# Loading q and k in 1 KB runs and putting the global keys inside the key chunks, in a banded attention followed by a hard-swish MLP

## The chip, the cores and the metric

The kernel runs on one core of a Trainium2 chip. The metric is device time in microseconds (us), the median of the executions of one kernel. An execution is also profiled; its span is about 1.7 us shorter than the device time of that same execution. The names of the engines are PE (TensorE, matmul), PEld (its weight loads), ACT (ScalarE), DVE (VectorE), POOL (GpSimd) and SP (SyncE, which here only issues DMA).

## The reference, cut to what matters

Eight batches, eight heads, 512 local positions and 32 global positions per head, head size 64. A local query sees all 32 global keys and the local keys within 32 positions of it. A global query sees all 544 keys. The attention's output (4352 rows of 512) goes through a two-layer MLP with 2048 hidden units, called MoE in the code and "expert" in some of the texts.

```python
s_g  = scale * q_g @ k_all.T                       # global queries: all keys
s_ll = where(|i - j| <= 32, scale * q_l @ k_l.T, -1e9)
s_lg = scale * q_l @ k_g.T
a_l  = softmax(concat(s_lg, s_ll));  out_l = a_l @ concat(v_g, v_l)
x    = concat(out_g, out_l)          # per batch: 544 rows of 512
h    = x @ w_in                      # 512 -> 2048
y    = (h * clip(h + 3, 0, 6) / 6) @ w_out
```

Inputs of the attention are drawn at 0.1 times a unit normal, so the scores are tiny and the softmax is nearly uniform. Some experiments below put rows in a wrong order on purpose; the comparison with the reference can't see that ("correct" there says nothing about order), and they serve for timing alone.

## The kernel before

One batch is four pairs of heads. For each pair the kernel transposes k and q on PE, copies them out of PSUM (k by DVE, q by ACT), computes band scores of four key blocks with query windows of 160, 192, 192 and 160 columns, and applies exp (ACT) and the band mask (DVE). A separate stage, once for two pairs, scores the global keys. Then V is applied, with the softmax's denominator in the upper 64 rows.

```python
def emit_T(p):
    ...                                            # 8 transposes by PE into psT (fp16 PSUM)
    nc.vector.tensor_copy(out=kT, in_=psT[:, 0:Sl])
    nc.scalar.copy(out=qT, in_=psT[:, Sl:2 * Sl])

def emit_G(Q):                                     # the global keys' score stage, two pairs at once
    for pp in range(2):
        nc.tensor.matmul(out=psA[:, 0:Sl], lhsT=kgz[:, b, m], rhs=st[p]["qT"], ...)
        nc.tensor.matmul(out=psB[:, 0:Sg], lhsT=kgz[:, b, m], rhs=qgT[:, m, b], ...)
    nc.scalar.activation(out=EG[:, 0:Sl], in_=psA[:, 0:Sl], func=EXP, scale=qk_scale)
    nc.scalar.activation(out=EG[:, Sl:S], in_=psB[:, 0:Sg], func=EXP, scale=qk_scale)
```

The MLP of one batch is cut into 32 units of work: 16 of the hidden layer (`u1`, tile `psH`, four matmuls of 512 columns each) and 16 of the output layer (`u2`, tile `po`). They fill PE while the next batch's attention waits for ACT and DVE. `M(n)` emits n of them.

```python
for p in range(NPAIR):
    ...
    emit_T(p + 2)
    M(1); emit_QK(p + 1); M(2); emit_G(...)        # G in every second pair
    M(2); emit_AV(p, lambda: M(1))
    if m == NM - 1:
        M(len(units))                              # finish this batch's units
        units += moe_units(...)                    # the next batch's 32
    else:
        M(2)
```

All PSUM tiles but one come from one pool of seven buffers. All loads of the local q, k and V are issued by POOL, and the DMA casts them from fp32 to fp16 on the way.

The softmax here doesn't subtract the row's maximum and nothing guards it: scores larger than these inputs give would overflow.

## Time and profile before

| | before |
|---|---|
| device time, median | 375.73 us (375.42 to 375.76) |
| span of the profiled execution, mean granted clock | 375.0 us, 0.986 |
| first matmul | 20.07 us |
| first hidden-layer matmul (psH); psH without gaps from | 44.7 us; 49.8 us |
| first output-layer matmul (po) | 70.4 us |
| one batch, psH to psH | 40.2 us: 20.9 hidden half + 19.3 output half |
| DMA packets | 114,272 |

I call "hidden half" the time from a batch's first psH matmul to its first po matmul, and "output half" the rest; both come from the timeline of PE.

The chain of waits, from the page of the kernel before (shares of the span, by engine and then by line; a q after an engine's name is its queue, "issue" is time in which it waited for nothing that the profile shows):

```profile
PE 62%; DVE 12%; POOL 9%; ACT 9%; issue 3%; DMA 3%; POOLq 0%
PE po L338 27%; PE psH L324 23%; PE pav L292 4%; ACT Rc L301 3%; DMA win_86<-in_moe_w_in_dram 3%; ACT Ln L298 3%; PE pav L284 2%; POOL kn L103 2%; POOL qn L103 2%; PE psGA L256 2%; POOL vn_81 L107 1%; POOL vgz L161 1%; PE pg L295 1%; POOL kn L96 1%; POOL qn L96 1%
```

PE's own MLP matmuls (po, psH) are half of it; POOL's issues (kn, qn, vn, vgz) are the start. The timeline of PE where the MLP begins (start, duration, engine, line, operation; in brackets the idle time before it and what ended it):

```profile
44.68 0.38 PE L324 MATMUL psH<-xt_324,win_84 128*128 128x512 f16 x1
45.93 0.39 PE L324 MATMUL psH<-xt_325,win_85 128*128 128x512 f16 x1 [0.87 <-DMA win_85<-in_moe_w_in_dram]
48.43 0.61 PE L324 MATMUL psH<-xt_326,win_86 128*128 128x512 f16 x1 [2.11 <-DMA win_86<-in_moe_w_in_dram]
```

The MLP is ready at 44.68 us and waits for the input weights. One batch of the steady part, by the windows view (window; its length; busy us and number of instructions of PE, PEld, DVE, ACT, POOL; granted clock; DMA share; GB/s):

```profile
130.00:170.20 40.20, 38.69 (x316) 20.57 (x313) 26.12 (x57) 28.46 (x56) 10.49 (x13) 1.00 0.69 66
```

PE is busy 38.69 of 40.20 us. It is the bound, with 1.5 us of idle time, and DVE and ACT have 14 and 12 us to spare over a whole batch. The groups that the change touches, with every shape apart (out<-in, shape, count; busy us, mean ns of one). A second group of 64 mask products (mask_79, 337 ns) is left out:

```profile
L244 DVE TENSOR_TENSOR E<-E,mask_80 128x352 f16<-128x352 f16 x64 | 20.9, 340 | 5.4 <-ACT E L242 3.4
L219 ACT COPY qT<-psT 128x512 f16<-128x512 f16 x32 | 18.8, 586 | 22.9 <-DVE kT L218 22.7
L218 DVE COPY kT<-psT 128x512 f16<-128x512 f16 x32 | 13.4, 418 | 2.9 <-PE psT L213 2.9
```

### The profile page before, as it was taken

Reading aid. Unit: us, or ns where it says so; the run is one execution under the profiler, and the core shown is the slowest. Engines: PE = TensorE matmul, PEld = TensorE weight load, DVE = VectorE, ACT = ScalarE, POOL = GpSimd, SP = SyncE. Lnnn points to the kernel's source line nnn. Section 1 sums busy time; section 2 is a strip of 40 time slices with the busy share of each in tenths; the row PEclk is TensorE's granted clock in tenths of the full one; section 3 lists DMA queues with packets and bytes.
Section 4 is the critical chain, followed back from the end, with each engine's and each line's share of the span. In section 5 each row is a group of like instructions: output and inputs, shape, how many; then the busy total and the mean of one; then the engine's idle time right before and its main releaser. Section 6 shows DMA issues by size and latency. Waiting matters only on the chain.

```text
span 375.0 us, 6707 instructions
## 1 busy us (share of the span) xinstructions
PE 332.3 (89%) x2608; PEld 178.9 (48%) x2608; DVE 235.6 (63%) x489; ACT 239.5 (64%) x473; POOL 102.6 (27%) x132
## 2 busy tenths in 40 slices
PE   0078589999999999999999999999999999999995
PEld 0046335555455554554555445545555445544472
DVE  7855667645875487548764587448754885296171
ACT  1059969745984599547965698458945895375070
POOL 8999436923240307003700343000000000000000
PEclk9998969999999999999999999999999999999999
DMA  9999999999390469119961949100001000100202
GB/s 131 120 77 141 199 204 169 152 131 84 44 101 29 75 67 110 32 58 86 68 47 56 114 27 86 50 36 30 2 30 56 30 2 28 58 28 0 87 29 56
DMA packets 114272, 27.44 MB, mean 73 GB/s; under 512 B 107328, under 2 KB 109376, under 8 KB 114240
## 3 DMA queue, kind: packets, MB, share of 16 engines
q0 software_dynamic: 104896, 17.05, 60.7%
q1 hardware_dynamic: 9344, 9.97, 7.9%
q8 instruction: 20, 0.33, 0.4%
q14 instruction: 12, 0.10, 0.1%
HBM read 35.13 MB, written 8.91 MB: 117 GB/s over the span
## 4 chain that ended last, share of the span: by engine, by line
PE 62%; DVE 12%; POOL 9%; ACT 9%; issue 3%; DMA 3%; POOLq 0%
PE po L338 27%; PE psH L324 23%; PE pav L292 4%; ACT Rc L301 3%; DMA win_86<-in_moe_w_in_dram 3%; ACT Ln L298 3%; PE pav L284 2%; POOL kn L103 2%; POOL qn L103 2%; PE psGA L256 2%; POOL vn_81 L107 1%; POOL vgz L161 1%; PE pg L295 1%; POOL kn L96 1%; POOL qn L96 1%
## 5 line engine op out<-in xcount | busy, mean ns | idle before, releaser
L298 ACT ACTIVATE Ln<-pav 64x512 f32<-64x512 f32 x64 | 37.9, 593 | 45.4 <-PE pav L292 38.1
L342 DVE COPY ot<-po 128x512 f32<-128x512 f32 x34 | 23.5, 692 | 25.6 <-PE po L338 25.2
L96 POOL DMA_DIRECT2D kn<-in_k_l_dram x28 | 24.7, 898 | 44.3 <-PE psT L213 36.5
L219 ACT COPY qT<-psT 128x512 f16<-128x512 f16 x32 | 18.8, 586 | 22.9 <-DVE kT L218 22.7
L96 POOL DMA_DIRECT2D qn<-in_q_l_dram x28 | 24.8, 926 | 6.7 <-PE psH L324 1.9
L284 PE MATMUL pav<-EG,vgz 128*128 128x512 f16 x64 | 24.7, 386 | 1.4 <-ACT qT L219 1.1
L244 DVE TENSOR_TENSOR E<-E,mask_79 128x352 f16<-128x352 f16 x64 | 19.8, 337 | 8.4 <-ACT E L242 8.2
L244 DVE TENSOR_TENSOR E<-E,mask_80 128x352 f16<-128x352 f16 x64 | 20.9, 340 | 5.4 <-ACT E L242 3.4
L324 PEld LDWEIGHTS <-win_86 128*128 128x128 f16 x144 | 14.2, 98 | 18.4 <-DMA win_86<-in_moe_w_in_dram 2.4
L324 PEld LDWEIGHTS <-win_87 128*128 128x128 f16 x144 | 14.1, 98 | 15.9 <-DMA win_87<-in_moe_w_in_dram 0.5
L301 ACT ACTIVATE Rc<-Ln 128x512 f32<-128x512 f32 x32 | 20.0, 626 | 0.7
L233 PEld LDWEIGHTS <-kT 64*128 64x128 f16 x256 | 13.6, 95 | 13.6 <-issue 13.1
L324 PEld LDWEIGHTS <-win_85 128*128 128x128 f16 x144 | 14.1, 98 | 11.0 <-issue 2.1
L112 POOL DMA_DIRECT2D vn_82<-in_v_l_dram x12 | 10.6, 918 | 31.4 <-PE pg L295 31.4
L190 PE MATMUL psGT<-ident,kgn_192 128*128 128x128 f16 x8 | 1.2, 304 | 20.1 <-DVE kgn_192 L183 20.1
L324 PEld LDWEIGHTS <-win_84 128*128 128x128 f16 x144 | 14.1, 98 | 9.8 <-issue 0.6
L238 PEld LDWEIGHTS <-kT 64*128 64x128 f16 x256 | 12.8, 94 | 6.7 <-issue 6.6
L218 DVE COPY kT<-psT 128x512 f16<-128x512 f16 x32 | 13.4, 418 | 2.9 <-PE psT L213 2.9
L286 PE MATMUL pg<-EG,vgz 128*128 128x32 f16 x64 | 10.8, 180 | 4.7 <-DVE xg_199 L314 4.7
L213 PE MATMUL psT<-ident,qn 128*128 128x128 f16 x128 | 12.9, 225 | 0.0
L112 POOL DMA_DIRECT2D vn_81<-in_v_l_dram x8 | 7.1, 909 | 21.1 <-PE pg L295 20.6
L213 PE MATMUL psT<-ident,kn 128*128 128x128 f16 x128 | 12.8, 225 | 0.0
(1097 smaller groups left out, 1112.3 us busy)
## 6 DMA issues: line engine op xcount, KB each, us to landing
out_dram<-ot SPq DMA_DIRECT2D x32, 256.0 KB, 2.0
kn<-in_k_l_dram POOLq DMA_DIRECT2D x28, 128.0 KB, 4.1
qn<-in_q_l_dram POOLq DMA_DIRECT2D x28, 128.0 KB, 5.3
vn_82<-in_v_l_dram POOLq DMA_DIRECT2D x12, 128.0 KB, 3.9
vn_83<-in_v_l_dram POOLq DMA_DIRECT2D x8, 128.0 KB, 5.1
vn_81<-in_v_l_dram POOLq DMA_DIRECT2D x8, 128.0 KB, 4.8
kgn<-in_k_g_dram SPq DMA_DIRECT2D x8, 64.0 KB, 2.7
kn<-in_k_l_dram POOLq DMA_DIRECT2D x8, 64.0 KB, 3.5
```

What stands on the lines that cost most here:

```text
L96: nc.gpsimd.dma_start(out=t[:, kb], in_=src[b, :, kb * P:(kb + 1) * P, :].rearrange("h s d -> s h d"))
L103: nc.gpsimd.dma_start(out=t[:, :, h], in_=src[b, h].rearrange("(kb p) d -> p kb d", p=P))
L112: nc.gpsimd.dma_start(out=vn[b % NV][:, kb, :, 0:D], in_=v_l[b, :, kb * P:(kb + 1) * P, :].rearrange("h s d -> s h d"))
L213: nc.tensor.matmul(out=psT[:, w * Sl + j * P:w * Sl + (j + 1) * P], lhsT=t[:, j, 2 * m:2 * m + 2].rearrange("p h d -> p (h d)"), rhs=ident ...
L219: nc.scalar.copy(out=qT, in_=psT[:, Sl:2 * Sl])
L244: nc.vector.tensor_tensor(out=E[:, e, half, 0:HALF], in0=E[:, e, half, 0:HALF], in1=mask[half], op=mult)
L284: nc.tensor.matmul(out=pav[:, 0:Sl], lhsT=vgz[:, b, h], rhs=EG[:, 0:Sl], start=True, stop=False, skip_group_check=True)
L298: nc.scalar.activation(out=Ln[e * D:(e + 1) * D], in_=pav[D:P, 0:Sl], func=LN)
L301: nc.scalar.activation(out=Rc, in_=Ln, func=EXP, scale=-1.0)
L324: nc.tensor.matmul(out=ps[:, 0:n], lhsT=w_in_t[m][:, c * P:(c + 1) * P], rhs=rhs(m), start=(m == 0), stop=(m == NM - 1))
L338: nc.tensor.matmul(out=po[t][:, 0:dm], lhsT=gts[c][:, t * P:(t + 1) * P], rhs=w_out_t[c // 4][:, c % 4], start=(c == 0), stop=(c == NC - 1))
L342: nc.vector.tensor_copy(out=ot, in_=po[t][:, 0:dm])
```

## The change

The intent is threefold. First, q and k are loaded as fp32 so that one partition reads four neighbouring rows, 1 KB in one run, in few DMA issues by SP, and are cast on chip; this is to bring the start forward. Row `4p + j` then lies in partition `p`, so the transposed copies out of PSUM have to put the rows back in order. Second, the keys are cut into five chunks of 128 with overlaps; chunk 1 holds the 32 global keys and serves queries 0 to 191, chunk 3 holds them again and serves queries 192 to 511, which ends the global score stage. Third, the global queries get one small 64-column matmul per chunk.

```diff
-        nc.vector.tensor_copy(out=kT, in_=psT[:, 0:Sl])
-        nc.scalar.copy(out=qT, in_=psT[:, Sl:2 * Sl])
+        nc.vector.tensor_copy(                      # the global keys, into two places of kT
+            out=kT[:, GC[0]:GC[0] + 2 * (GC[1] - GC[0])].rearrange(...)[:, :, 0:Sg],
+            in_=kgT[b % 2][:, m:m + 1].to_broadcast([P, 2, Sg]))
+        kv = psT[:, 0:Sl].rearrange("d (j p) -> d j p", j=J)            # J = 4
+        for k0, k1, c0 in SEG:                      # three pieces: 128, 160, 224 keys
+            nc.vector.tensor_copy(
+                out=kT[:, c0:c0 + k1 - k0].rearrange("d (p j) -> d j p", j=J),
+                in_=kv[:, :, k0 // J:k1 // J])
+        nc.scalar.copy(
+            out=qT.rearrange("d (p j) -> d j p", j=J),
+            in_=psT[:, Sl:2 * Sl].rearrange("d (j p) -> d j p", j=J))
 ... (scores)
+    CH = [(0, 0, 0, 160), (Sg, 128, 0, 192), (0, 160, 192, 128), (Sg, 288, 192, 320),
+          (0, 384, 352, 160)]            # globals in the chunk, first key, first query, queries
+        for c in range(NCH):
+            nc.tensor.matmul(out=psG[:, c * 2 * Sg:(c + 1) * 2 * Sg],
+                             lhsT=kT[:, KC[c]:KC[c] + P], rhs=qgz[b % 2][:, m])
 ... (emit_G is gone; the E masks have 480 columns instead of 352; Eg gets a mask of 128)
 ... (start)
+    for m in range(2):
+        for i, src in enumerate((k_l, q_l)):
+            load_rows(nc.sync, nat[0][0][i], src[0], 2 * m, 2)          # fp32, by SP
+        if m == 0:
+            load_g(0, gf0)
+    load_v0(0)                                                          # V as fp32, by SP
+    ...
+    for i in range(4):
+        load_w_in(i)                                                    # by POOL, at once
 ... (loop)
+        if b + 1 < B:                                # casts of the next batch: POOL, after the start
+            cast_rows(b + 1, m, first if b == 0 and m < 2 else pool)
```

## The prediction

> **What bounds the kernel now.** Granted clock 0.986, span 375.0 us, split by the first MoE matmuls of each batch (timeline of PE).
> - Start, 0 to about 50 us. PE does nothing until 20.07 us. The chain of waits runs there through POOL's DMA issues (kn, qn, vn: 0.69 to 0.74 us each, one after another); then batch 0's attention keeps ACT busy without a gap from 22.0 to 47.8 us, and the first MoE matmuls wait for win (11.94 us). The dense stream begins at 49.8 us.
> - Middle: one batch takes 40.2 us (psH of consecutive batches at 129.99 and 170.2). 512-column matmuls start every 0.216 us. By start times PE needs 128 x 0.216 = 27.65 for the MoE and, per pair, 0.45 (transposes) + 0.43 (scores; the two heads run side by side) + 0.24 (global scores) + 1.30 (AV) = 2.42: 37.3 in all. The other 2.9 us are stalls, mostly in the hidden half (20.9 us against 19.35 for the output half), where PE waits for DVE (gt, xg).
> - Tail: 45 us of pure MoE from 329.7 us, unchanged.
>
> **What the change does, costed.**
> 1. Start: q and k of two heads come in a few issues not made by POOL, V as fp32 likewise; win is queued at once. First exp near 9 us instead of 25. ACT then still needs, with start-to-start times from the trace (E 0.40 for 416 columns, so 0.45 for 480; qT 0.47; Ln 0.6; Rc 0.52) plus query casts, 23 to 25 us (kgz's 3.3 us are gone). DVE needs about as much. Dense MoE from 36 us (32 to 41): 14 us earlier, all on the critical path. Some 2 us more may come back in batch 0's hidden half, which runs now among win waits and a reduced clock (PEclk 0.83 at 40 to 60 us).
> 2. PE per pair: global scores 0.24 become five 64-column matmuls (0.14) and 0.05 of transposes; scores 0.43 to 0.41; AV 1.30 to 1.08 (960 columns against 1216). 2.42 becomes 2.13: 1.15 us a batch.
> 3. Added to DVE: the kT copy (418 ns) becomes three copies with an 8-byte step plus one of the global keys. The Trainium skill ("VectorE: DVE Perf Modes", "Mode 2×_1P") asks for 16-bit data at step 1; the trace agrees for the dense copy (418 ns against 692 for fp32). So 1x: an estimate of 1.0 + 0.2 us. Masks 352 to 480 columns: 0.34 to 0.40 each, plus one Eg mask of 0.2. DVE rises from 26 to 31 us a batch; in the hidden half it is nearly full, so it returns part of step 2.
> 4. POOL gets eight casts a batch, which share SBUF ports with DVE (the skill, "SBUF — State Buffer", "Who interferes with whom"). POOL has 28 us free a batch, so no wait for casts.
> 5. ACT: EG (0.62 + 0.24 per two pairs) out, Eg and wider E in: even.
>
> Net period 39.3 us (38.4 to 40.5): 6 us saved. DMA packets fall to about half.
>
> **Predicted**: 36 + 40.8 + 6 x 39.2 + 45.3 = 357 us, range 347 to 368. Faster by over 2%: 0.88; within 2%: 0.09; slower: 0.03.
>
> **What would show it.** First PE matmul near 7 us; dense psH from about 36 us, then batches 39.3 us apart; kT pieces 0.3 to 0.4 us each; E masks 0.40 us; DVE near 31 us per batch; POOL never on the chain after 40 us.
>
> **What would make it wrong.** Win loads starving the first k, q or V loads; POOL casts taking several us or blocking DVE's masks; DVE becoming the bound so the period stays at 40; or a start quicker than ACT's sum.

## The result, and the profile after

The changed kernel took 392.25 us (median, 391.86 to 392.92, 4 executions) against 375.75 us of the kernel before in the same rounds. The ratio is 1.0437, 95% interval 1.0413 to 1.046: slower. Ratios in this document are the mean time of one kernel's runs over that of the kernel before's of the same rounds, so they are not quite the ratios of the medians quoted.

| us | before | predicted | after |
|---|---|---|---|
| first matmul | 20.07 | 7 | 11.73 |
| first exp | 25.31 | 9 | 18.72 |
| first psH | 44.7 | 36 | 51.2 |
| from there to the next batch's psH | 45.1 | 40.8 | 45.8 |
| then six batches | 238.6 | 235.2 | 246.6 |
| rest | 46.6 | 45.3 | 46.9 |
| one steady batch | 40.2 | 39.3 | 41.5 |

The columns of measured pieces add up to the spans, 375.0 and 390.5. The prediction's pieces add up to 357.3, so it missed by 33 us: 15 until the first psH, 5 until the next batch's, 11 in the six batches and 2 in the rest. Against the kernel before, 7.2 us are lost until the second psH and 8.0 us in the six batches after it. The second loss is the plainer one. One batch of the steady part, windows view of the changed kernel:

```profile
138.50:180.00 41.50, 39.20 (x312) 21.31 (x310) 30.98 (x74) 32.34 (x58) 11.12 (x18) 1.00 0.51 95
```

DVE is 4.9 us busier in a batch, as predicted (31), but ACT is 3.9 us busier too, where "even" was predicted. The groups, with every shape apart:

```profile
L245 DVE TENSOR_TENSOR E<-E,mask 128x480 f16<-128x480 f16 x128 | 53.6, 439 | 17.9 <-ACT E L244 16.8
L215 ACT COPY qT<-psT 128x512 f16<-128x512 f16 x32 | 41.8, 1305 | 13.2 <-DVE kT L212 12.5 <-DVE mask L176 0.7
L212 DVE COPY kT<-psT 128x224 f16<-128x224 f16 x32 | 22.3, 697 | 0.0
L212 DVE COPY kT<-psT 128x160 f16<-128x160 f16 x32 | 17.6, 551 | 0.0
L212 DVE COPY kT<-psT 128x128 f16<-128x128 f16 x32 | 14.0, 439 | 5.2 <-PE psT L202 5.2
```

The same 512 elements of qT take 1305 ns instead of 586, four times a batch: 2.9 us of ACT's 3.9. The three kT pieces take 1.69 us together instead of 0.42.

The chain of waits of the changed kernel:

```profile
PE 41%; ACT 20%; DVE 17%; DMA 11%; issue 5%; SPq 5%; POOL 0%; ACTq 0%
PE po L317 28%; DMA gz_79<-in_k_g_dram 6%; PE psH L302 6%; DVE kT L212 4%; ACT qT L215 4%; ACT Ln L276 4%; SPq L137 4%; PE pav L272 3%; DVE gt L308 3%; DMA qf<-in_q_l_dram 3%; ACT Rc L279 2%; DMA vf<-in_v_l_dram 2%; ACT E L244 1%; SPq L94 1%; PE psT L202 1%
```

POOL has left the chain, as intended, but PE fell from 62% to 41%, with kT and qT copies and several loads in its place (gz are the global keys and queries, qf and vf are q and V as fp32). Three moments of the start show the loads (timelines of ACT, of POOL, and of PE):

```profile
4.34 0.62 ACT L125 CAST qr_142<-qf 128x512 f16<-128x512 f32 x1 [2.25 <-DMA qf<-in_q_l_dram]
15.26 0.62 ACT L125 CAST qr_147<-qf 128x512 f16<-128x512 f32 x1 [10.30 <-DMA qf<-in_q_l_dram]
...
18.72 0.52 ACT L242 ACTIVATE Eg<-psG 128x320 f16<-128x320 f32 x1
```

```profile
23.68 0.99 POOL L140 CAST vn_84<-vf 128x640 f16<-128x640 f32 x1 [17.96 <-DMA vf<-in_v_l_dram]
```

```profile
65.75 0.45 PE L187 MATMUL psGT<-ident,gz_79 128*128 128x32 f16 x8 [2.88 <-DMA gz_79<-in_k_g_dram]
```

The first q cast ran at 4.34 us, but the second, issued by SP at 3.30, waited until 15.26, and V until 23.68. Meanwhile the four win loads, queued by POOL from 1.35 us on, took their share. At 62.9 us PE, in the middle of a hidden half, stopped for the global keys of batch 2, which had been issued at 41.48 us behind the output weights and landed 24.2 us later.

### The profile page after: what moved, and what is told of

It is laid out like the page before. It is cut to its first block, busy times and chain, and to the rows that moved or that the text cites. A ratio compares the mean times of both kernels' runs of the same rounds, so it can differ in the third digit from the quotient of the medians.

```text
span 390.5 us, 6834 instructions
## 1 busy us (share of the span) xinstructions
PE 337.8 (87%) x2560; PEld 186.0 (48%) x2560; DVE 273.8 (70%) x628; ACT 270.4 (69%) x479; POOL 86.4 (22%) x134
## 2 busy tenths in 40 slices
DMA packets 72274, 36.82 MB, mean 94 GB/s; under 512 B 47408, under 2 KB 67888, under 8 KB 72240
## 4 chain that ended last, share of the span: by engine, by line
PE 41%; ACT 20%; DVE 17%; DMA 11%; issue 5%; SPq 5%; POOL 0%; ACTq 0%
PE po L317 28%; DMA gz_79<-in_k_g_dram 6%; PE psH L302 6%; DVE kT L212 4%; ACT qT L215 4%; ACT Ln L276 4%; SPq L137 4%; PE pav L272 3%; DVE gt L308 3%; DMA qf<-in_q_l_dram 3%; ACT Rc L279 2%; DMA vf<-in_v_l_dram 2%; ACT E L244 1%; SPq L94 1%; PE psT L202 1%
## 5 line engine op out<-in xcount | busy, mean ns | idle before, releaser
L317 PEld LDWEIGHTS <-gt 128*128 128x128 f16 x544 | 49.4, 97 | 54.1 <-issue 2.5
L245 DVE TENSOR_TENSOR E<-E,mask 128x480 f16<-128x480 f16 x128 | 53.6, 439 | 17.9 <-ACT E L244 16.8
L215 ACT COPY qT<-psT 128x512 f16<-128x512 f16 x32 | 41.8, 1305 | 13.2 <-DVE kT L212 12.5
L212 DVE COPY kT<-psT 128x128 f16<-128x128 f16 (+2 forms) x96 | 41.4, 562 | 5.2 <-PE psT L202 5.2
L317 PE MATMUL po<-wout_91,gt 128*128 128x512 f16 x136 | 35.0, 379 | 0.0
L317 PE MATMUL po<-wout_90,gt 128*128 128x512 f16 x136 | 34.9, 379 | 0.0
L317 PE MATMUL po<-wout_93,gt 128*128 128x512 f16 x136 | 34.9, 379 | 0.0
L317 PE MATMUL po<-wout_92,gt 128*128 128x512 f16 x136 | 34.9, 378 | 0.0
L239 PEld LDWEIGHTS <-kT 64*128 64x128 f16 x320 | 14.7, 98 | 24.8 <-issue 15.8
L242 ACT ACTIVATE Eg<-psG 128x320 f16<-128x320 f32 x32 | 14.1, 439 | 12.5 <-PE psG L229 12.4
L272 PE MATMUL pav<-E,vn_84 128*128 128x160 f16 (+3 forms) x160 | 22.1, 274 | 0.0
L272 PE MATMUL pav<-E,vn_85 128*128 128x160 f16 (+3 forms) x160 | 20.3, 244 | 0.0
L302 PEld LDWEIGHTS <-win_89 128*128 128x128 f16 x144 | 13.6, 98 | 13.6 <-issue 1.6
L272 PEld LDWEIGHTS <-vn_84 128*128 128x128 f16 x160 | 15.9, 108 | 7.9 <-issue 1.1
L302 PEld LDWEIGHTS <-win_86 128*128 128x128 f16 x144 | 13.5, 98 | 12.9 <-issue 0.9
L302 PEld LDWEIGHTS <-win_87 128*128 128x128 f16 x144 | 13.6, 98 | 12.0
L302 PEld LDWEIGHTS <-win_88 128*128 128x128 f16 x144 | 13.1, 97 | 12.2 <-issue 0.2
L274 PE MATMUL pg<-Eg,vn_84 128*128 128x32 f16 x160 | 13.3, 181 | 6.3 <-DVE vn_84 L140 4.3
L272 PEld LDWEIGHTS <-vn_85 128*128 128x128 f16 x160 | 14.7, 97 | 6.9
```

The source lines that it names most:

```text
L212: nc.vector.tensor_copy(out=kT[:, c0:c0 + k1 - k0].rearrange("d (p j) -> d j p", j=J), in_=kv[:, :, k0 // J:k1 // J])
L215: nc.scalar.copy(out=qT.rearrange("d (p j) -> d j p", j=J), in_=psT[:, Sl:2 * Sl].rearrange("d (j p) -> d j p", j=J))
L239: nc.tensor.matmul(out=pss[e][:, c0:c0 + nq], lhsT=kT[r, KC[c]:KC[c] + P], rhs=qT[r, q0:q0 + nq])
L242: nc.scalar.activation(out=Eg, in_=psG[:, 0:NCH * 2 * Sg], func=EXP, scale=qk_scale)
L245: nc.vector.tensor_tensor(out=E[:, e, t], in0=E[:, e, t], in1=mask[:, t], op=mult)
L272: nc.tensor.matmul(out=pav[:, q0:q0 + nq], lhsT=lhs, rhs=E[:, e, t, c0:c0 + nq], start=(i == 0), stop=(i == NCH - 1), skip_group_check=True)
```

## The experiments

Theory 1 (steady part): the loss of 1.3 us a batch comes from the copies that *write* SBUF with an 8-byte step. Its rivals are the wider masks, the casts on POOL, and the new matmul order. Theory 2 (start): the loads are bound by the DMA engines and in the wrong order. Its rivals are the clock, the dearer copies, and POOL's casts.

All results in one table (four executions each; "O" is the first po matmul, "batch" one steady batch; both from the profiled execution, which need not be the median one):

| run | median us | ratio to before, 95% | first psH | O | batch |
|---|---|---|---|---|---|
| after | 392.25 | 1.0437 (1.0413 to 1.046) | 51.2 | 77.5 | 41.5 |
| x_dense | 387.33 | 1.0315 (1.027 to 1.0359) | 45.9 | 78.5 | 40.4 |
| x_kdense | 389.57 | 1.0358 (1.0317 to 1.0399) | 50.0 | 78.2 | 41.0 |
| x_qdense | 387.56 | 1.0303 (1.0268 to 1.0338) | 48.8 | 77.5 | 40.7 |
| x_readstride | 386.16 | 1.0261 (1.0206 to 1.0317) | 48.0 | 79.3 | 40.3 |
| y_before_scatter | 393.22 | 1.0475 (1.0441 to 1.0509) | 51.9 | 74.1 | 42.1 |
| x_gz3 | 395.47 | 1.0506 (1.0448 to 1.0564) | 52.4 | 81.3 | 41.5 |
| x_read_gz3 | 377.87 | 1.0061 (1.0016 to 1.0105) | 46.8 | 70.6 | 40.3 |
| x_hold | 385.11 | 1.0272 (1.0208 to 1.0335) | 44.3 | 74.8 | 41.5 |
| x_hold_nopool | 385.48 | 1.0269 (1.0206 to 1.0333) | 45.6 | 69.8 | 41.5 |
| x_read_hold | 375.39 | 0.9985 (0.9942 to 1.0027) | 47.0 | 68.6 | 40.3 |
| x_read_hold_c1 | 376.09 | 1.001 (0.9961 to 1.006) | 48.2 | 70.5 | 40.3 |
| x_read_hold_c1_carry | 371.52 | 0.9892 (0.9867 to 0.9916) | 45.5 | 67.8 | 39.7 |
| x_first | 376.08 | 1.0025 (0.9977 to 1.0073) | 39.0 | 69.1 | 40.3 |
| x_first_split | 371.1 | 0.9885 (0.9853 to 0.9917) | 44.0 | 70.3 | 39.4 |
| x_first_split_carry | 368.19 | 0.9802 (0.9774 to 0.9831) | 44.2 | 69.8 | 39.1 |
| y_before_split | 368.11 | 0.9784 (0.9746 to 0.9822) | 45.0 | 67.3 | 39.0 |
| y_before_split_carry | 366.07 | 0.9749 (0.9722 to 0.9776) | 44.9 | 68.7 | 38.8 |

### Which side of the copy carries the step

x_dense writes and reads both copies densely. The rows then stand in the wrong order.

```diff
-                out=kT[:, c0:c0 + k1 - k0].rearrange("d (p j) -> d j p", j=J),
-                in_=kv[:, :, k0 // J:k1 // J])
+                out=kT[:, c0:c0 + k1 - k0], in_=psT[:, k0:k1])
-            out=qT.rearrange("d (p j) -> d j p", j=J), in_=psT[...].rearrange("d (j p) -> d j p", j=J))
+            out=qT, in_=psT[:, Sl:2 * Sl])
```

> The kernel after, with the kT and qT copies written densely, so the rows come out in the wrong order: the result is wrong on purpose. Nothing else changes. Theory S (the scattered 2-byte writes at an 8-byte step are what lengthened the period from 40.2 to 41.5 us): qT falls from 1.305 to 0.59 us, the three kT pieces from 1.69 us in all to about 0.8 us, the batch period to 39.3 to 39.7 us, the time from 392 to about 375 us (about 14 us in the middle, 2 to 3 us in the start). Rival W (the wider masks, POOL's casts on the shared port, or the smaller PSUM slack are the cause): the copies get shorter but the period stays above 41 us and the time above 387 us.

x_kdense and x_qdense do so for one copy alone.

> The changed kernel with the three kT pieces of VectorE written densely and ScalarE's qT copy still scattered (row order wrong on purpose). Theory V (VectorE's scattered pieces, about 1.2 us a pair dearer, lengthen the batch): period 41.5 to 40.4 to 40.7, as with both dense, time 386 to 389. Theory A (ScalarE's qT, 0.7 us a pair dearer, which the scores wait for): period stays 41.2 to 41.5, time 390 to 392.

> The changed kernel with ScalarE's qT copy written densely and VectorE's kT pieces still scattered (row order wrong on purpose). Theory V: period stays 41.2 to 41.5, time 390 to 392. Theory A: period 40.4 to 40.7, time 386 to 389. If both lie on one path, each gives about half: 40.8 to 41.1 in both runs.

x_readstride keeps the right order, but walks the elements in the order in which they are written: SBUF is written densely and PSUM is read with a step of 256 bytes.

```diff
-        kv = psT[:, 0:Sl].rearrange("d (j p) -> d j p", j=J)
+        kv = psT[:, 0:Sl].rearrange("d (j p) -> d p j", j=J)
-                out=kT[...].rearrange("d (p j) -> d j p", j=J), in_=kv[:, :, k0 // J:k1 // J])
+                out=kT[...].rearrange("d (p j) -> d p j", j=J), in_=kv[:, k0 // J:k1 // J])
-            out=qT.rearrange("d (p j) -> d j p", j=J), in_=psT[...].rearrange("d (j p) -> d j p", j=J))
+            out=qT.rearrange("d (p j) -> d p j", j=J), in_=psT[...].rearrange("d (j p) -> d p j", j=J))
```

> The kernel after, with the row order restored on the reading side: the copies read PSUM at a 256-byte step and write SBUF densely. The result is right. If the cost lies in the scattered 2-byte writes: qT 0.59 us, kT pieces 0.3 to 0.4 us (1x rate), period 39.6 to 40.2 us, time 377 to 382 us. If any step on either side costs the same: qT stays at 1.3 us and the time at 392 us.

y_before_scatter gives the kernel before the stepped writes and nothing else (order wrong).

```diff
-        nc.vector.tensor_copy(out=kT, in_=psT[:, 0:Sl])
-        nc.scalar.copy(out=qT, in_=psT[:, Sl:2 * Sl])
+        nc.vector.tensor_copy(out=kT.rearrange("d (p j) -> d j p", j=NT), in_=psT[:, 0:Sl].rearrange("d (j p) -> d j p", j=NT))
+        nc.scalar.copy(out=qT.rearrange("d (p j) -> d j p", j=NT), in_=psT[:, Sl:2 * Sl].rearrange("d (j p) -> d j p", j=NT))
```

> The kernel before with nothing changed but the kT and qT copies, which now write with the 8-byte step of the kernel after (the row order is wrong on purpose). Theory S: qT 1.3 us and kT about 1.4 us each instead of 0.59 and 0.42; the period goes from 40.2 to 41.3 us or more, the start grows by 4 to 6 us (ACT works without a gap there and gets 0.57 us more per pair), the time from 376 to 385 to 392 us. If the period of the kernel after came from its other parts: the copies get slower but the time stays within 379 us.

The steady batch fell from 41.5 us to 40.4 with both copies dense, and to 40.3 with stepped reads and dense writes. One copy alone gave 0.5 us (k) and 0.8 us (q), which together is a little more than both did: theory V was wrong, and theory A does not account for k's 0.5 us. It is nearest to the third case named there, both copies on one path, with q's share the larger. In the other direction, stepped writes alone lengthened the batch of the kernel before from 40.2 to 42.1 us and its time by 17.8 us. So the stepped writes account for the steady loss: without them it goes, and with them alone it comes; masks, POOL casts and matmul order were all still there in x_readstride. The times were forecast less well. x_dense was to take about 375 us and x_readstride 377 to 382, and they took 387.33 and 386.16: the copies' share of the start (the first psH 5.3 us earlier in x_dense) was lost again before the first po, where PE waited 6.3 us (x_dense) and 8.5 us (x_readstride) for global keys. The groups of x_readstride, then of x_dense (k only), then of y_before_scatter:

```profile
L215 ACT COPY qT<-psT 128x512 f16<-128x512 f16 x32 | 19.1, 596 | 1.5 <-DVE kT L212 0.3
L212 DVE COPY kT<-psT 128x224 f16<-128x224 f16 x32 | 12.1, 378 | 0.0
L212 DVE COPY kT<-psT 128x128 f16<-128x128 f16 x32 | 9.0, 282 | 4.3 <-PE psT L202 4.3
```

```profile
L212 DVE COPY kT<-psT 128x224 f16<-128x224 f16 x32 | 8.4, 262 | 0.0
L212 DVE COPY kT<-psT 128x128 f16<-128x128 f16 x32 | 6.9, 215 | 2.0 <-PE psT L202 2.0
```

```profile
L220 ACT COPY qT<-psT 128x512 f16<-128x512 f16 x32 | 41.5, 1304 | 22.7 <-DVE kT L218 22.6
L218 DVE COPY kT<-psT 128x512 f16<-128x512 f16 x32 | 41.4, 1293 | 4.5 <-PE psT L213 4.5
```

From two lengths of one copy the cost of one element follows without the fixed part. On DVE it is (262 - 215)/96 = 0.49 ns with both sides dense, (378 - 282)/96 = 1.0 ns with a stepped read, and (697 - 439)/96 = 2.7 ns with a stepped write. The Trainium skill ("VectorE: DVE Perf Modes", "Mode 2×_1P") asks for 16-bit data at step 1 for two results a cycle; the first two numbers agree with it, a factor of two. The third does not come from that rule: it is another 2.7 times. ACT reads with the step at no cost (596 ns against 588 dense) and pays 1305 for the stepped write.

### Order of the loads at the start

x_hold makes the weights and batch 1's V wait for batch 0's V. A one-element write by POOL into each of those tiles reads V's fp32 tile, so the loads, which overwrite the element, can't be issued earlier. No wait is taken away.

```diff
     def load_w_in(i):
+        nc.gpsimd.tensor_copy(out=w_in_t[i][:, 0, 0:1], in_=vf[:, NCH - 1, 0, 0:1])
         nc.gpsimd.dma_start(out=w_in_t[i], ...)
     def load_w_out(i):
+        nc.gpsimd.tensor_copy(out=w_out_t[i][:, 0, 0:1], in_=vf[:, NCH - 1, 0, 0:1])
     def load_v(b):
+        if b == 1:
+            nc.gpsimd.tensor_copy(out=vn[1][:, :, 0, 0:1], in_=vf[:, :, 0, 0:1])
```

> The kernel after, with the loads of win, wout and batch 1's V held back until the first V chunk of batch 0 has landed (one element of each is written from that chunk first). Theory D (the start is late because win, queued at once, takes the DMA engines from q, k, V and the global keys): the first global keys land at about 6 us instead of 11, the second q at about 8 instead of 15.3, the first exp starts at 9 to 11 us instead of 18.7, and the dense MoE stream begins near 45 to 50 us instead of 66 us; with the period at 41.5 us the time is 372 to 380 us. Rival C (the start is set by ACT and DVE work, mostly the slow copies, and the data's lateness is hidden behind it): the first exp comes earlier but the dense stream begins no earlier than 60 us and the time stays above 385 us.

The first matmul moved from 11.73 to 6.79 us, the first exp from 18.72 to 12.26, the first psH from 51.2 to 44.3, and the time fell by 7.1 us. Nothing but the order of the loads had changed, and before V landed in the changed kernel (23.68 us) POOL had issued no load but win, so the win loads had been starving q, k and V. That is theory D's mechanism, with its size missed: the time of 385.11 us, against the 372 to 380 expected, lies in the range named for rival C. In this the Trainium skill ("DMA: Bandwidth & Descriptors", "Issuing engines are not separate DMA queues") agrees: the loads of SP and of POOL share the same 16 engines, so queueing win "at once" was not free.

x_read_hold joins the edits of x_readstride and of x_hold, shown above.

> The kernel after with both repairs: stepped reads with dense writes, and the loads of win, wout and batch 1's V held back. Result right. If the two gains add: 392 - 6 - 7 = 379 us, with the period at 40.3 us and the first output half at about 68 us. If the late start is now set by POOL's casts blocking DVE's mask products (two products took 5.4 us in the held-back kernel, ending when a row of casts ended), the first hidden half stays near 29 us long and the time is 380 to 383 us.

It ran in 375.39 us, level with the kernel before. The two edits alone gave 6.1 and 7.1 us and together 16.9: more than the sum, and more than either expectation (379, or 380 to 383) allowed. The start's stops seem to hide one another; the next two runs show such a case.

x_gz3 gives the global keys a third buffer and loads batch 2's before the output weights, to take away the stop at 62.9 us.

```diff
-gz = [const(f"gz{i}", [P, 2, H, D]) for i in range(2)]
+gz = [const(f"gz{i}", [P, 2, H, D]) for i in range(3)]
     load_g(1)
+    load_g(2)
     load_v(1)
 ...
-            load_g(b + 1)
+            if b + 2 < B:
+                load_g(b + 2)
```

> The kernel after with a third buffer for the global keys and queries, so that batch 2's are loaded ahead of wout instead of behind it. Theory D predicts that PE's stop at 62.9 to 66.2 us (transposes waiting for global keys that took 24 us to land) goes and the time falls by 2 to 4 us, to 388 to 390 us. If another load or engine would have stopped PE there anyway: no change.

x_read_gz3 is the same edit on x_readstride.

> As the run that steps the PSUM reads and writes densely (386.2 us, TensorE waited 8.5 us for batch 2's global keys at 60 to 70 us), with a third buffer for the global keys, so that batch 2's are loaded before the output weights. Theory G (that wait is what the start still loses): wait gone, first output matmul at 70 to 73 instead of 79.3, time 378 to 381. Rival (another stop takes its place, as in the run with the third buffer alone): time 384 to 387.

In the changed kernel alone this took the wait away and gave nothing: 395.47 us (three executions near 395.5, one of 391.85), against 388 to 390 expected. Two mask products then took 5.74 us and PE waited 4.6 us for what came behind them. With the copies mended, where PE had waited longer for these keys (8.5 us), the same edit took 8.3 us off, from 386.16 to 377.87. PE's waits between 45 and 82 us in x_readstride, then between 36 and 82 us in x_read_gz3 (who waited, for whom: us in total, times, longest):

```profile
PE psGT L187 <- DMA gz<-in_k_g_dram: 8.5, 1, 8.5
```

```profile
PE psS L240 <- ACT qT L216: 3.2, 3, 2.3
PE psT L203 <- DVE kr L125: 1.7, 1, 1.7
PE psS L240 <- DVE gt L309: 0.6, 2, 0.3
```

So two repairs, the write side of two copies and the place of two 32 KB loads, undo 14.4 of the 16.5 us.

### POOL casts beside DVE's mask products

In the profiled execution of x_hold, two stretches of DVE are long (timeline of DVE, then the first and last casts of the row on POOL beside the second):

```profile
61.11 3.30 DVE L247 TENSOR_TENSOR E<-E,mask 128x480 f16<-128x480 f16 x2
64.73 5.38 DVE L247 TENSOR_TENSOR E<-E,mask 128x480 f16<-128x480 f16 x2
```

```profile
65.35 0.62 POOL L125 CAST kr<-kf 128x512 f16<-128x512 f32 x1
...
69.25 0.60 POOL L125 CAST qr<-qf 128x512 f16<-128x512 f32 x1
```

Two products take 0.72 us elsewhere. These took 5.38, of which the second alone 5.06, and ended 0.3 us after the row of eight casts did; PE waited 5.1 us behind them. The Trainium skill ("SBUF — State Buffer", "Who interferes with whom") says that a VectorE instruction with two SBUF inputs contends with a GpSimd instruction that reads SBUF. x_hold_nopool takes these casts from POOL in the first batches.

```diff
-            cast_rows(b + 1, m, first if b == 0 and m < 2 else pool)
+            cast_rows(b + 1, m, first if b <= 2 else pool)
```

> As the run with the weights held back (385.1 us), whose trace had two mask products of 3.30 and 5.38 us for the pair beside rows of GpSimd casts, and a TensorE wait of 5.1 us behind the second. Here the casts of batches 1 to 3 go to VectorE and ScalarE. Theory L (the casts hold VectorE's products of two SBUF tiles): no pair of masks over 1.6 us before 80 us, the 5.1 us wait gone, first output matmul at 69 to 72 instead of 74.8, time 380 to 383. Rival (the long masks come from something else, or another stop takes the place): masks still over 3 us, or time 384 to 387.

No pair of masks before 80 us took over 0.79 us, PE's wait was gone and the first po came at 69.8 instead of 74.8 us:

```profile
63.86 0.73 DVE L247 TENSOR_TENSOR E<-E,mask 128x480 f16<-128x480 f16 x2
64.64 0.41 DVE L247 TENSOR_TENSOR E<-E,mask 128x480 f16<-128x480 f16 x1
```

That supports the mechanism. The time, though, did not fall: 385.48 us against 385.11, in the range named for the rival (384 to 387), so the size was wrong. Two reasons can be read from the runs. The profiled execution of x_hold was its slowest (388.81; the others 384.11 to 385.6), so a median execution very likely did not have the whole stop. And the casts now load DVE and ACT, so that the next half was longer (20.8 us for the first output half, against 18.9). How often the stop happens was not measured, since each run has one profiled execution. But it is no oddity of x_hold: of the 15 kept traces of the changed kernel and its versions, seven have a single mask product of over 2 us (2.1 to 5.1), the changed kernel's own among them (2.67 us at 68.6 us), and none of the four traces of the kernel before and its versions has. In x_gz3, with one of 5.01 us, the profiled execution (395.51 us) is like two of the other three, so there the median may well contain it.

x_read_hold_c1 is x_read_hold with one buffer instead of two for the cast tiles, which keeps POOL from casting two batches in one row.

```diff
-        r[m] = [natp.tile([P, J, 2, D], FP16, tag=f"{t}{m}", name=f"{t}{m}") for t in ("kr", "qr")]
+        r[m] = [natp.tile([P, J, 2, D], FP16, tag=f"{t}{m}", name=f"{t}{m}", bufs=1) for t in ("kr", "qr")]
```

> The one before it with one buffer instead of two for each cast q and k tile, so that POOL can no longer cast two batches in one row. Theory P (rows of POOL casts keep DVE's products of two SBUF tiles waiting): no E mask product over 1 us, the first hidden half 4 to 8 us shorter, time 372 to 376 us. If the port is not the cause: mask products of several us remain, or the half stays as long; no change.

It changed nothing (376.09 against 375.39, intervals overlapping). x_read_hold had no pair of masks above 1.6 us to begin with, so this run decides nothing about the casts.

### What still held the start

In x_read_hold the longest wait of PE between 36 and 72 us was this:

```profile
PE psT L204 <- POOL kr L125: 11.1, 1, 11.1
```

The cast stood in POOL's queue behind loads whose issue waited for earlier transfers. x_first is x_read_hold with all of batch 1's casts given to DVE and ACT.

```diff
-            cast_rows(b + 1, m, first if b == 0 and m < 2 else pool)
+            cast_rows(b + 1, m, first if b == 0 else pool)
```

> As the run with the dense-write copies and the held-back weights (375.4 us), but the casts of batch 1 go to VectorE and ScalarE instead of GpSimd. In that run TensorE waited 11.1 us (36 to 47 us) for one GpSimd cast that stood in GpSimd's queue behind loads waiting for earlier transfers. Theory Q (the in-order GpSimd queue sets the start of the dense stage): first expert matmul at 38 to 41 us instead of 47, first output matmul at 60 to 64 instead of 68.6, period unchanged at 40.3, time 367 to 371 us. Theory B (DMA bandwidth sets it: the loads of the weights and of batch 1 are not there earlier): at most 3 us less, 372 to 376 us.

The first psH came at 39.0 us as theory Q said, and the time did not move (376.08): the first hidden half became 30.1 us long instead of 21.6, and the first po stayed at 69.1 us. PE now waited for batch 1's V:

```profile
PE pav L274 <- DMA vn<-in_v_l_dram: 5.0, 1, 5.0
```

Theory B is nearer: batch 1's data and the weights are not there earlier. In x_first the DMA engines moved 14.40 MB in the first 60 us, and the DMA row of its page (busy tenths in slices of 9.4 us) begins 8999999. That a still better order could gain is not excluded; none was tried.

A second loss at the start is the granted clock. In x_hold it was 0.50 from 30 to 45 us and 0.53 from 70 to 75, after the 5.1 us wait; in x_first it was 0.50 from 25 to 30 and from 35 to 40 us. The Trainium skill ("TensorE: Matmul & The Clock Gate", "What's actually happening") describes half clock when PE has been idle. The window after the 5.1 us wait agrees; from 30 to 45 us PE was not idle but thinly fed (busy 3.52, 2.78 and 4.13 us of each 5, at the low clock). That an earlier start with a thinly fed PE gives part of its gain back is an inference; no run separates it.

### The order of work, in both kernels

PE's work was predicted 1.15 us a batch smaller, and no version with the order of work unchanged went below 40.3 us. In the hidden half of x_first PE stood in the score block, which asks for five of the pool's seven PSUM buffers at once (timeline of PE, x_first):

```profile
129.82 0.31 PE L231 MATMUL psG<-qgz,kT 128*128 128x64 f16 x5
130.06 0.58 PE L241 MATMUL psS<-qT,kT 64*128 64x160 f16 x8
131.27 0.45 PE L276 MATMUL pg<-Eg,vn 128*128 128x32 f16 x8 [0.63 <-DVE xg L294]
131.66 0.38 PE L241 MATMUL psS<-qT,kT 64*128 64x320 f16 x2
131.97 0.24 PE L276 MATMUL pg<-Eg,vn 128*128 128x32 f16 x3
132.06 2.32 PE L304 MATMUL psH<-xt,win 128*128 128x512 f16 x10
```

From 129.82 to 132.06 is 2.24 us. x_first_split emits the block in two parts with two MLP units between them; x_first_split_carry also leaves four units of a batch over for the next one's border. The same two edits were made to the kernel before (y_before_split, y_before_split_carry).

```diff
-    def emit_QK(p):
+    def emit_QK(p, mid=None):
     ...                                   # after the first half's exp and masks:
+                if mid: mid()
-            emit_QK(p + 1)
-        M(4)
+            emit_QK(p + 1, lambda: M(2))
+        M(2)
     ...
-            M(len(units))
+            M(len(units) - 4)             # _carry only
```

> As the run before it in this list, with the score block emitted in two parts and two expert units between them, so that it asks for three PSUM buffers at once and not five of seven. Theory P (the score block's claim on PSUM stalls TensorE by about 1.4 us in each of the two score blocks of the hidden half): hidden half 21.3 to about 20.3 us or less, period 40.3 to 39.3 us, 5 to 8 us less time. Theory T (the throughput of ScalarE and VectorE limits the hidden half): period stays 40.2 to 40.4, time within 2 us of that run.

> As the run before it in this list, with four expert units of each batch carried over the batch's border, where the attention's result for the next expert stage is waited for. Theory of the border stall: 0.7 us less per batch, as the same carry gave in an earlier run (40.3 to 39.6), so another 4 to 6 us in all; if the split has already filled the border, under 2 us.

> The one before it with four output units of the MoE kept over to the next batch's first pair. Theory A (the hidden half is held by ACT, which works 19 of 21.3 us there, and by the wait for xt at the batch's border): the border stall of about 1.5 us a batch is filled, period 38.7 to 39.4 us, time 6 to 10 us less than the one before it. If PE were the limit: no change.

> The kernel before with the split score block alone, no carried units. The pair of rules gave 366.1 us and a period of 38.8. If the split gives most of it, as in the changed kernel (5 of 8 us): period 39.0 to 39.4, 368 to 370 us. If the carry does: period 39.6 to 40.0, 371 to 374 us.

> The kernel before, with the same split of the score block and the same carry of four units, so that the gain of the order is not credited to the change. If both rules of order work as well there: period 40.2 to 38.8 to 39.5 us and time 366 to 371 us. If its order is already limited by the engines: within 2 us of 375.7.

The same block in x_first_split:

```profile
129.75 0.31 PE L231 MATMUL psG<-qgz,kT 128*128 128x64 f16 x5
129.98 0.38 PE L241 MATMUL psS<-qT,kT 64*128 64x160 f16 x6
130.30 1.90 PE L306 MATMUL psH<-xt,win 128*128 128x512 f16 x8
132.13 0.38 PE L241 MATMUL psS<-qT,kT 64*128 64x320 f16 x4
132.44 1.90 PE L306 MATMUL psH<-xt,win 128*128 128x512 f16 x8
```

The two parts cost 0.55 and 0.31 us. The batch fell to 39.4 us and the time by 5.0 us, at the lower edge of what theory P said. Its mechanism, the claim on the pool, is not shown by this. In the block above, the one idle time that the trace names (0.63 us) is for xg of DVE, which reads `pg`, the one PSUM tile outside the pool; the split lets MLP units run before that point, and this block fell from 2.24 to 0.86 us. The other block of the hidden half, whose named waits are for gt and xt of DVE (they read pool tiles), fell only from 2.25 to 2.13 us. In the kernel before, too, the longest wait of a batch is that of pg for xg (0.8 us), and after its split it is gone. The wait for pg is thus a rival that these runs do not separate from the buffers. The carry took a further 2.9 us here, less than the 4 to 6 expected, and 4.6 us where the split was absent (x_read_hold_c1_carry against x_read_hold_c1): the two edits fill in part the same idle time.

The kernel before gained more: 8.2 us from the split alone against the kernel before of the same rounds (368.11 and 376.3), and 366.07 with both, which is the fastest version, 2.5% under the kernel before. The windows of one batch of x_first_split_carry and of y_before_split_carry (the two halves in one window each):

```profile
167.80:188.10 20.30, 19.62 (x160) 10.52 (x159) 17.45 (x42) 18.99 (x37) 3.44 (x6) 1.00 0.26 39
188.10:206.90 18.80, 18.80 (x152) 9.94 (x151) 12.10 (x33) 10.79 (x24) 7.67 (x11) 1.00 0.50 56
```

```profile
166.40:185.80 19.40, 19.40 (x157) 10.01 (x156) 15.07 (x29) 17.77 (x34) 7.00 (x8) 1.00 0.92 80
185.80:205.20 19.40, 19.40 (x157) 10.04 (x156) 10.85 (x28) 10.40 (x24) 3.50 (x4) 1.00 0.49 58
```

The reordered kernel before has no PE idle time at all: 38.80 busy of 38.80 us. The reordered changed kernel has 38.42 of 39.1, but its busy time is no measure of its work, since the modelled ends of matmuls cover part of the waits. The output halves show the work: PE is busy throughout in both kernels, for 18.8 us against 19.4, 0.6 us less for two pairs. The hidden half has two pairs as well and 0.2 us of transposed global keys, so by estimate it needs 19.0 us, also 0.4 us less than before, and the change saves PE some 1.0 us of work a batch, near the 1.15 predicted. But the hidden half takes 20.3 us: 1.3 us of waiting, in which ACT is busy 18.99 us, give more than that back. With the same order in both, and in the same rounds, the changed kernel is still 2.1 us slower (368.19 against 366.07).

By start-to-start times of PE in these two traces, applying V went from 5.2 to 4.3 us a batch, 0.21 us a pair where 0.22 was predicted. The scores went from 3.4 to 4.7 us, some of which is still waiting. Undisturbed, the two score parts of a pair cost 0.86 us (0.55 + 0.31 above), and those of the kernel before 0.30 + 0.30 + 0.245 (half of the global stage) = 0.845 us: no saving where 0.12 us was predicted, for five chunks of 960 columns per head took the place of four of 704. The transposed global keys add 0.2 us.

No run moves the reorder to the DMA or to PE.

## Why the prediction was wrong, point by point

- **"So 1x: an estimate of 1.0 + 0.2 us" for the kT copies: mis-sized.** The mechanism, that the step takes DVE out of its two-a-cycle mode, was right for the read side: stepped reads cost 282 + 313 + 378 ns = 0.97 us in x_readstride, nearly the 1.0 predicted. The change steps the write side, and that took 1.69 us. The total of DVE (31 us a batch) was right all the same, by luck: other terms of that sum had been put too high.
- **"ACT: ... even": wrong, and the larger term.** The stepped qT copy was seen in the diff but priced as the old one. It went from 586 to 1305 ns, 2.9 us a batch on ACT, and was worth 0.8 us of each batch (x_qdense).
- **"PE per pair ... 1.15 us a batch": near in size (1.0 us by the estimate above), but it did not shorten the batch.** The V part came as predicted and the score matmuls themselves saved nothing. The account of the kernel before was off as well: it gave PE 37.3 us of need and 2.9 of stalls, but the reordered kernel before keeps PE busy for 38.8. The step that failed is the next one, that PE's saved work becomes a shorter period.
- **"Net period 39.3": wrong.** It was 41.5. With the copies mended 40.3, so even then the saving was not there: the output half was shorter (19.0 us, before 19.3), but the hidden half was 21.3 us (before 20.9), with PE waiting in the score blocks. Only with the order changed as well did the period reach 39.1, and the kernel before then reached 38.8.
- **"Dense MoE from 36 us": wrong.** I summed ACT's work and took it for the bound of the start. What bound it was when loads landed, and that sum itself was too small by the stepped copies (x_dense, with dense copies and the loads as they were, had its first psH 5.3 us earlier). The prediction's own list of dangers had it ("Win loads starving the first k, q or V loads"), but gave it no time. x_hold alone brought 7 us back at the first psH. The other danger on the list, POOL casts blocking masks, was real in the traces; taking the casts away from POOL in x_hold did not lower the median.
- **"No wait for casts": wrong at the start.** POOL had time, but works in order: in x_read_hold a cast stood behind loads and PE lost 11.1 us.
- **Right:** masks near 0.40 us (the median; the mean is 439 ns), POOL off the chain of waits, the tail unchanged in substance (46.9 against 46.6 us). The packets fell by 37%, to 72,274, and not by half, and that bought no time: POOL's issues had left the chain, but at the start the DMA engines were as full as before (the first eight slices of the pages' DMA rows read 89999999, before 99999999). The packets carry more as well, 36.82 MB against 27.44, as q and k now land in SBUF as fp32.

What stays open: how often POOL's casts hold DVE in an unprofiled execution, whether the split worked through the pool's buffers or through the wait for pg, why the second score block of the hidden half still waits after it, and whether another order of loads at the start would gain.

## What to carry to other kernels

When a layout change forces a reordering copy, put the step on the PSUM read and write SBUF densely, and price the copy on every engine that does one, ACT too. Before crediting an earlier start, list which loads must land by then and what shares the DMA engines with them; a load queued "at once" delays those that are needed first. And where a fused kernel's PE waits in bursts although it is the bound, try the order of emission (a block split in two with other work between, units carried over a border) before removing work: here it was worth 9 us to the old kernel, and no version of the change measured here ran as fast.

## What the Trainium skill lacked or had wrong

- "SBUF — State Buffer" (section "Door 1: The DMA port swizzle") says that accesses with at least two hits in each 16-byte line run at full bandwidth, and gives 8 bf16 as how far one can stride for free. Here 2-byte writes with an 8-byte step, two in each such line, took 1305 ns instead of 586 for 512 elements on ScalarE, and 2.7 ns an element on VectorE instead of 0.49 dense. Either that rule does not hold for engine writes of 16-bit data, or something else limits them; the measurement decides.
- No page that I read gives the cost of stepped PSUM reads by ScalarE and VectorE. "SBUF — State Buffer" says only that non-contiguous PSUM access slows matmuls. Reads at a 256-byte step cost ScalarE nothing (596 ns against 588) and VectorE the loss of the two-a-cycle mode alone (1.0 ns an element against 0.49).
- "SBUF — State Buffer" ("Who interferes with whom") describes an exclusive lock for the length of an instruction. The runs agree on who contends, but a row of back-to-back GpSimd casts of 0.6 us each held one mask product for 5.06 us, until 0.3 us after the row had ended; the page does not say that the waiting VectorE instruction fails to get in between two of them.
